# Layer two's first pair of blocks: one second product behind each first one, and x's parts apart from x's sums

## The chip, the cores and the metric

The kernel runs on one core of a Trainium2 chip. The metric is the device time of one execution in microseconds, as the median of several runs; less is better. A separate execution was recorded by the hardware profiler, and its own time is given beside its span. The engines of a core are TensorE (in the rows PE; its weight loads PEld), VectorE (DVE), ScalarE (ACT), GpSimd (POOL) and SyncE (SP, which issues the transfers here). Each engine works through its own queue in the order in which the program issues; engines wait for one another by semaphores.

## The reference

A retention layer makes x (1536 tokens by 512), and two layers of two matrices each follow. Layer one bends with a softplus, layer two with a scaled square:

```python
x = retention(q, k, v)                       # 1536 x 512
h = x @ w_in;  g = maximum(h, 0) + log1p(exp(-abs(h)));  x = g @ w_out
h = x @ w2_in; r = maximum(h, 0); g = s * (r * r) + b;   out = g @ w2_out
```

The widths are 512 (x) and 2048 (h), so a layer has 16 blocks of 128 columns of h. All is float32.

## The kernel before

**Precision.** A float32 operand is cut into a high and a low part (`split`, L107 to L114: ScalarE copies to the high part, L111; GpSimd or VectorE subtracts it, L114), and a product is made of three matmuls, high by high, high by low and low by high. The tokens are cut into three tiles j of 512; x's parts are `xh[j]`, `xl[j]` and its plain float32 copy, or what is kept in its place, `xa[j]`. A weight half comes as 64-bit words; `split_w` makes it into float32 on VectorE in four steps (L286, L290, L295, L301) with a square on ScalarE (L293, "wm"), and then cuts it into `wh` (ScalarE, L111) and `wl` (GpSimd, L114). It is a generator: `go(work, n)` runs its next n steps, so that a slot of the program does one weight half: two steps early in the slot, the rest at its end. Loads of weights are issued from the third step, four buffers ahead.

**Layer one** runs in 48 steps s (a first product `h_mm` of 12 matmuls into bank h or y, the softplus on VectorE and ScalarE, and, LAG = 3 steps later, the second product `acc_mm` of 12 matmuls into four accumulator banks). At the end of the steps the second products of blocks 45, 46 and 47 are still to do, all of tile j = 2, and then x's tile 2 is finished by `take_last`, for two banks at a time: VectorE adds `xa` to the accumulators in place (L416), ScalarE writes `xh` from them (L418), and VectorE writes `xl` (L420).

**Layer two** works on pairs p of blocks. From the second pair on (`second`, p >= 1), tiles 0 and 1 of x are multiplied by a scheme with seven products in the place of eight (`six`, 6 matmuls each). It needs sums of x's parts, T1 = B12 - B11, T2 = B22 - T1, T3 = B22 - B12 (made before T2) and N4 = B21 - T2, cut into high and low parts, and sums of the weights: four differences on GpSimd (L320, "ws"), their high part on ScalarE (L111, "sh") and low part on GpSimd (L114, "sl"). They are a slot's work (`sums_w`) like a weight half: the four differences in its first two steps, sh and sl in the third. A product that stays in a bank while another is made in the same bank is copied out by ScalarE (`kept`, L469, p1, p5 and u2). Buffers p1 and p5 hold T3 before that, one copy of each.

**The first pair** (`plain(0)`) makes its six products plainly, in six slots (j, half): (0,0), (0,1), (1,0), (1,1), (2,0), (2,1). A slot issues, in this order: the first product (`all_of`, 12 matmuls on TensorE into the bank named in its call), the relu on ScalarE (`flat`, L486), square (L492), affine (L493) and high part gh (L111) on ScalarE with the low part gl on GpSimd (L114), the first two steps of its split work, then `accs()` (second products on TensorE, and what reads the accumulators), the sums of x, and the rest of the split work. The split works of the slots are, in order: a weight half of block 19, the weight sums of the second pair, two weight halves, and a weight half each of blocks 20 and 21. `acc_2(p, j, half)` is a second product (12 matmuls) into the four accumulator banks; the first of a tile takes new accumulators and so waits for what still reads the old ones, bank by bank (banks 0 and 1 are one buffer, 2 and 3 one each). `take` moves a tile's accumulators to `xa[j]` with four VectorE instructions (L518 for the first pair, L520 later).

Before the change, `mixed_x(k)` does a sum of x on VectorE (L446, L431, L441) and its parts on ScalarE (L447, or L111 for T3) and GpSimd (L449, or L114) at one place, T3 and N4 excepted, whose parts come in later slots: T1 and T3's sum in the last step of layer one, T2 in slot (0,0), N4's sum in (0,1) and parts in (1,1), T3's parts in (2,0). The second products stand so: blocks 45 and 46 in slot (0,0); 47 and `take_last` in (0,1); the first pair's own second products of tile 0 in (1,0) and (1,1), with `take`; none in (2,0) and (2,1). The order of TensorE's queue is therefore (0,0), 45, 46, (0,1), 47, (1,0), second product of (0,0), (1,1), second product of (0,1), (2,0), (2,1). The order on every engine is the order in which the program is written; nothing reorders it (`tc.manual_schedule()`).

Of the kernel before, what the change touches and what calls it, by code (L numbers as in the profile page):

```python
# [7 lines left out]
F32 = mybir.dt.float32  # L8
F32R = mybir.dt.float32r
U32 = mybir.dt.uint32  # L10
AF = mybir.ActivationFunctionType
ALU = mybir.AluOpType

P = 128
# [7 lines left out]
TT = 512  # L22
# [10 lines left out]
FIRST, SECOND = (0, 1), (2, 3)  # L33
LAG = 3
# [13 lines left out]
def tile_retention_mlps(ctx: ExitStack, tc: tile.TileContext, qk, kv, w1, w2, sb, consts, out):  # L48
# [19 lines left out]
    def bank(pool, tag):  # L68
        return pool.tile([P, 512], F32, tag=tag, name=tag)
# [39 lines left out]
    def split(hi, lo, src, hi_eng, lo_eng):  # L109
        if hi_eng is nc.scalar:  # L110
            nc.scalar.activation(hi, src, AF.Copy)  # L111
        else:
            hi_eng.tensor_copy(hi, src)
        lo_eng.tensor_tensor(out=lo, in0=src, in1=hi.bitcast(F32), op=ALU.subtract)  # L114
# [269 lines left out]
    def acc_mm(s, banks):  # L384
        la, g, j, f4 = steps[s]
        wh, wl = w_t[block(s), 1]
        gh, gl = gg_t[s]
        if (la, g, j) not in acc_t:
            acc_t[la, g, j] = sums()[0] if acc_t else ac
        parts = ((0, 1), (2,)) if len(banks) > 1 else ((0, 1, 2),)  # L390
        for some in parts:
            for cc in banks:
                cs = slice(cc * P, (cc + 1) * P)
                ops = ((wh[:, cs], gh), (wh[:, cs], gl), (wl[:, cs], gh))
                for i in some:
                    nc.tensor.matmul(  # L396
                        acc_t[la, g, j][cc], *ops[i], start=f4 == 0 and i == 0, stop=ends(s) and i == 2
                    )
# [23 lines left out]
    x_t = {}  # L422
    x3 = []

    def mixed_x(k):

        (b11, b21), (b12, b22) = ((xa[j][:, 0:2], xa[j][:, 2:4]) for j in (0, 1))
        if k == 3:
            for c, tag in enumerate(("p1", "p5")):
                t = late.tile([P, TT], F32, tag=tag, name=tag)  # L430
                nc.vector.tensor_tensor(out=t, in0=b22[:, c], in1=b12[:, c], op=ALU.subtract)  # L431
                x3.append(t)
            return
        if k == 4:
            hi, lo = xh[1][:, 0:2], xl[1][:, 0:2]
            for c in range(2):
                split(hi[:, c], lo[:, c], x3[c], nc.scalar, nc.gpsimd)
            x_t[3] = hi, lo
            return
        if k == 5:  # L440
            nc.vector.tensor_tensor(out=b12, in0=b21, in1=b22, op=ALU.subtract)  # L441
            return
        to, x, y = {1: (b11, b12, b11), 2: (b22, b22, b11), 0: (b12, None, None)}[k]
        hi, lo = (late.tile([P, 2, TT], F32R, tag=f"x{k}{e}", name=f"x{k}{e}") for e in "hl")
        if x is not None:
            nc.vector.tensor_tensor(out=to, in0=x, in1=y, op=ALU.subtract)  # L446
        nc.scalar.activation(hi, to, AF.Copy)  # L447
        for c in range(2):
            nc.gpsimd.tensor_tensor(out=lo[:, c], in0=to[:, c], in1=hi[:, c].bitcast(F32), op=ALU.subtract)  # L449
        x_t[k] = hi, lo  # L450

    def six(ps, w, x, start):
# [48 lines left out]
    def acc_2(p, j, half, banks=FIRST + SECOND):  # L501
        wh, wl = w_t[NF + 2 * p + half, 1]
        gh, gl = gg_t[p, half, j]
        if (1, p, j) not in acc_t:
            acc_t[1, p, j] = sums()[0]
        for some in ((0, 1), (2,)):
            for cc in banks:
                cs = slice(cc * P, (cc + 1) * P)
                ops = ((gh[:, cs], wh), (gl[:, cs], wh), (gh[:, cs], wl))
                for i in some:  # L510
                    nc.tensor.matmul(  # L511
                        acc_t[1, p, j][cc], *ops[i], start=half == 0 and i == 0, stop=half == 1 and i == 2
                    )
# [112 lines left out]
    with tc.manual_schedule():  # L626
# [90 lines left out]
        for s in range(SB, NS):  # L717
            old = s - LAG
            takes = ends(old)
            late_work = work  # L720
            work = split_next(s + 1) if not takes else iter(())
            h_mm(s)
            act_0(s)
            if s > SB:
                act_3(s - 1)
            go(work, 2)
            acc_mm(old, FIRST)
            if takes:
                take_out(old, 0)
                take_out(old, 1)  # L730
            act_1(s)
            if s > SB:
                act_hi(s - 1)
            act_2(s)
            go(late_work, 1)
            if s > SB:
                act_lo(s - 1)
            acc_mm(old, SECOND)
            if takes:
                take_out(old, 2)  # L740
                take_out(old, 3)
            for k in SUMS_AT.get(s, ()):
                mixed_x(k)
            go(work, 2)

        def part(p):
# [6 lines left out]
        def plain(p):  # L753

            w = NF + 2 * p

            def slot(j, half, to, accs, sums=()):
                work = part(p)
                all_of(to, w_t[w + half, 0], j)
                c = flat(to)  # L760
                bend(c, p, half, j)
                go(work, 2)
                accs()
                for k in sums:
                    mixed_x(k)
                go(work, 3)

            def last():
                for s in range(NS - LAG, NS - 1):
                    acc_mm(s, FIRST + SECOND)  # L770

            def end():
                for banks in (FIRST, SECOND):
                    acc_mm(NS - 1, banks)
                    take_last(banks)

            def sums_0():
                acc_2(p, 0, 1)
                take(p, 0)

            slot(0, 0, bank(ps_h, "h"), last, (2,))
            slot(0, 1, bank(ps_y, "y"), end, (5,))
            slot(1, 0, bank_2[1], lambda: acc_2(p, 0, 0))
            slot(1, 1, bank(ps_h, "h"), sums_0, (0,))
            slot(2, 0, bank_2[1], lambda: None, (4,))
            slot(2, 1, bank(ps_y, "y"), lambda: None)

        def second(p):

            w = NF + 2 * p  # L790
            (ah, al), (bh, bl), (sh, sl) = w_t[w, 0], w_t[w + 1, 0], s_t[w]
            a11, a12 = (ah[:, :KH], al[:, :KH]), (ah[:, KH:], al[:, KH:])
            a22 = bh[:, KH:], bl[:, KH:]
            s1, s2, s3, s4 = ((sh[:, k], sl[:, k]) for k in range(4))
            b11, b21 = ((xh[0][:, k : k + 2], xl[0][:, k : k + 2]) for k in (0, 2))
            b22 = xh[1][:, 2:4], xl[1][:, 2:4]
            t1, t2, t3, n4 = (x_t[k] for k in (1, 2, 3, 0))

            one, other, third = bank(ps_h, "h"), bank(ps_y, "y"), bank_2[1]

            work = part(p)
            six(one, a11, b11, True)
            p1 = kept(one, "p1")
            six(third, a12, b21, True)
            c11 = joined(third, p1)
            go(work, 2)
            acc_2(p - 1, 1, 0)
            bend(c11, p, 0, 0)
            go(work, 3)

            work = part(p)
            six(other, s1, t1, True)
            p5 = kept(other, "p5")
            six(one, s2, t2, False)
            u2 = kept(one, "u2")
            go(work, 2)
            acc_2(p - 1, 1, 1)
            take(p - 1, 1)
            go(work, 3)

            work = part(p)
            six(other, s4, b22, False)
            c12 = joined(other, u2)
            six(one, s3, t3, False)
            c22 = joined(one, p5)
            go(work, 2)
            acc_2(p - 1, 2, 0)
            bend(c12, p, 0, 1)
            bend(c22, p, 1, 1)
            go(work, 3)  # L830

            work = part(p)
            six(one, a22, n4, False)
            c21 = flat(one)
            go(work, 2)
            acc_2(p - 1, 2, 1)
            take(p - 1, 2)
            bend(c21, p, 1, 0)
            go(work, 3)

            work = part(p)
            all_of(third, (ah, al), 2)
            ha = flat(third)
            go(work, 2)
            acc_2(p, 0, 0)
            bend(ha, p, 0, 2)
            go(work, 3)

            other = bank(ps_y, "y")
            all_of(other, (bh, bl), 2)  # L850
            hb = flat(other)
            for banks in (FIRST, SECOND) if p == PAIRS - 1 else (FIRST + SECOND,):
                acc_2(p, 0, 1, banks)
                take(p, 0, banks)
            bend(hb, p, 1, 2)
# [85 lines left out]
```

## Time and profile before

| | |
|---|---|
| median of 3 runs | 585.06 us (584.42 to 586.7) |
| profiled execution | 585.04 us, span on the core 583.2 us |
| mean granted TensorE clock | 0.994 of full |
| busy: TensorE, weight loads | 98%, 80% |
| busy: VectorE, ScalarE, GpSimd | 72%, 54%, 41% |

The span is the profiled stretch on the core; the execution's time has some 1.8 us around it. Times in the rows count from the span's start. An instruction's row has its start, its length, its engine and line, what it writes and reads, and in brackets how long the engine was idle before it and what ended that. TensorE's matmuls overlap in the rows: a row says 0.39 us, but they start closer together than that. A row with x2 or x4 merges so many instructions in a line. The second pair (p = 1) begins behind slot (2,1), at about 345 us.

### The profile page before, as it was taken

To read this page: it belongs to the slowest core of one execution; us is meant where nothing else is said; L and a number is where in the kernel's file an instruction comes from. 1 tells how busy PE (TensorE), PEld (TensorE's weight loads), DVE (VectorE), ACT (ScalarE), POOL (GpSimd) and SP (SyncE) were. 2 spreads that over 40 slices of the span, in tenths; PEclk is the share of its full clock that TensorE was granted. 3 is DMA by queue.
4 is the path that set the end of the run, shared out by engine and by line. 5 is a ranking of instruction groups with operands and counts; after the bars stand their busy time and mean duration, and the time that the engine had idled before them with its cause. 6 is when DMAs were issued, how large, how long until landed. Compare 5 with 4: busy or idle time off the path is not lost.

```text
span 583.2 us, 7949 instructions
## 1 busy us (share of the span) xinstructions
PE 569.2 (98%) x2986; PEld 467.2 (80%) x2986; DVE 419.8 (72%) x626; ACT 316.6 (54%) x570; POOL 236.3 (41%) x197
## 2 busy tenths in 40 slices
PE   8999999999999999999999798999999999999997
PEld 7877778888888888888888586888888888888885
DVE  4899766788799997999869775749394857653324
ACT  3656564444233233243435776958677676767460
POOL 3447632111110120120525777665747464735030
PEclk9999999999999999999999898999999999999999
DMA  8986212122122131122121131403021222000005
GB/s 322 415 316 199 69 53 93 46 100 62 48 73 67 50 100 37 52 93 72 38 72 37 36 97 53 141 0 114 33 95 50 72 73 72 2 1 0 1 1 215
DMA packets 14869, 50.57 MB, mean 87 GB/s; under 512 B 1776, under 2 KB 1776, under 8 KB 14832
## 3 DMA queue, kind: packets, MB, share of 16 engines
q1 hardware_dynamic: 14832, 50.08, 25.0%
q8 instruction: 23, 0.38, 0.3%
q14 instruction: 14, 0.11, 0.1%
HBM read 46.93 MB, written 3.15 MB: 86 GB/s over the span
## 4 chain that ended last, share of the span: by engine, by line
PE 84%; DVE 6%; DMA 5%; ACT 3%; issue 1%; SPq 0%; DVEq 0%
PE acc L511 22%; PE acc L396 21%; PE h L349 12%; PE y L349 9%; PE h L455 7%; PE y L463 3%; PE third L463 3%; PE y L455 3%; DMA qk<-qk 3%; PE y L189 2%; DMA raw<-w 2%; PE third L455 1%; PE s L173 1%; DVE wm L301 1%; DVE xa L446 1%
## 5 line engine op out<-in xcount | busy, mean ns | idle before, releaser
L114 POOL TENSOR_TENSOR wl<-wm,wh 128x512 fp32r<-128x512 f32 x64 | 83.3, 1302 | 223.0 <-ACT wh L111 223.0
L520 DVE TENSOR_TENSOR xa<-acc,xa 128x512 f32<-128x512 f32 x84 | 52.4, 684 | 81.8 <-PE acc L511 81.8
L114 POOL TENSOR_TENSOR gl<-c,gh 128x512 fp32r<-128x512 f32 x48 | 62.1, 1294 | 77.6 <-ACT gh L111 64.0
L362 ACT ACTIVATE t<-t 128x512 f32<-128x512 f32 x48 | 30.2, 629 | 102.9 <-DVE t L356 102.8
L511 PE MATMUL acc<-wh,gh 128*128 128x512 f32 x192 | 76.0, 396 | 3.7 <-DVE xl L420 3.7
L396 PE MATMUL acc<-gh,wh 128*128 128x512 f32 x192 | 75.6, 394 | 0.0
L511 PE MATMUL acc<-wh,gl 128*128 128x512 f32 x192 | 75.4, 393 | 0.0
L396 PE MATMUL acc<-gl,wh 128*128 128x512 f32 x192 | 74.8, 390 | 0.0
L111 ACT ACTIVATE wh<-wm 128x512 fp32r<-128x512 f32 x64 | 39.8, 622 | 49.9 <-DVE wm L301 49.9
L396 PE MATMUL acc<-gh,wl 128*128 128x512 f32 x192 | 58.1, 389 | 0.0
L511 PE MATMUL acc<-wl,gh 128*128 128x512 f32 x192 | 53.0, 392 | 0.0
L382 DVE TENSOR_TENSOR gl<-t,gh 128x512 fp32r<-128x512 f32 x40 | 52.1, 1302 | 1.2 <-ACT gh L378 1.2
L349 PE MATMUL h<-xh,wh 128*128 128x512 f32 x112 | 44.7, 399 | 2.3 <-DVE t L366 1.7
L293 ACT ACTIVATE wm<-raw 128x512 f32<-128x512 f32 x64 | 42.2, 660 | 8.5 <-POOL wl L114 8.4
L511 PEld LDWEIGHTS acc<-wh,gh 128*128 128x128 f32 x192 | 36.6, 190 | 12.5 <-issue 3.4
L349 PE MATMUL h<-xl,wh 128*128 128x512 f32 x112 | 43.7, 390 | 0.0
L396 PEld LDWEIGHTS acc<-gh,wh 128*128 128x128 f32 x192 | 36.1, 188 | 8.8 <-DVE xa L406 1.0
L511 PEld LDWEIGHTS acc<-wl,gh 128*128 128x128 f32 x192 | 36.6, 190 | 7.7
L511 PEld LDWEIGHTS acc<-wh,gl 128*128 128x128 f32 x192 | 36.6, 191 | 7.6
L396 PEld LDWEIGHTS acc<-gh,wl 128*128 128x128 f32 x192 | 36.0, 188 | 7.6
L396 PEld LDWEIGHTS acc<-gl,wh 128*128 128x128 f32 x192 | 36.0, 188 | 7.2
L493 ACT ACTIVATE c<-c,sbt 128x512 f32<-128x512 f32 x48 | 39.2, 816 | 1.6
(179 smaller groups left out, 1237.6 us busy)
## 6 DMA issues: line engine op xcount, KB each, us to landing
raw<-w SPq DMA_DIRECT2D x64, 512.0 KB, 3.7
qk<-qk SPq DMA_DIRECT2D x12, 512.0 KB, 8.2
kv<-kv SPq DMA_DIRECT2D x12, 512.0 KB, 8.1
out<-xa SPq DMA_DIRECT2D x12, 256.0 KB, 2.1
cst<-consts SPq DMA_DIRECT2D x1, 518.0 KB, 4.2
cst<-consts SPq DMA_DIRECT2D x1, 256.0 KB, 6.4
sbt<-sb SPq DMA_DIRECT2D x1, 1.0 KB, 9.7
```

The source lines that it names most:

```text
L111: nc.scalar.activation(hi, src, AF.Copy)
L114: lo_eng.tensor_tensor(out=lo, in0=src, in1=hi.bitcast(F32), op=ALU.subtract)
L293: nc.scalar.activation(m, hw.bitcast(F32), AF.Square)
L349: nc.tensor.matmul(ps, w[:, cc * P : (cc + 1) * P], r[j][:, cc, :], start=i == 0, stop=i == len(ops) - 1)
L362: nc.scalar.activation(l_t[s], l_t[s], AF.Softplus)
L382: (eng or nc.vector).tensor_tensor(out=gl, in0=l_t.pop(s), in1=gh.bitcast(F32), op=ALU.subtract)
L396: nc.tensor.matmul(acc_t[la, g, j][cc], *ops[i], start=f4 == 0 and i == 0, stop=ends(s) and i == 2)
L455: nc.tensor.matmul(ps, w[a][:, k * P : (k + 1) * P], x[b][:, k], start=start and i == 0, stop=i == len(ops) - 1, skip_group_check=True,)
L463: nc.tensor.matmul(ps, w[a][:, k * P : (k + 1) * P], (xh, xl)[b][j][:, k], start=i == 0, stop=i == len(ops) - 1)
L493: nc.scalar.activation(c, c, AF.Identity, scale=sbt[:, 0:1], bias=sbt[:, 1:2])
L511: nc.tensor.matmul(acc_t[1, p, j][cc], *ops[i], start=half == 0 and i == 0, stop=half == 1 and i == 2)
L520: nc.vector.tensor_tensor(out=dst, in0=ps, in1=dst, op=ALU.add)
```

## The change

`mixed_x` is cut into `sum_x` (VectorE alone) and `parts_x` (ScalarE and GpSimd). In the last step of layer one only the sums T1 and T3 stay. In the six slots the second products are spread to one each: block 45 in (0,0), 46 in (0,1), 47 with `take_last` in (1,0), the first pair's second products of tile 0 in (1,1) and, with `take`, in (2,0), none in (2,1). T2's sum stays in (0,0), N4's in (0,1). The parts go: T1 to (0,0), T2 to (0,1), N4 to (1,1), T3 to (2,1). The banks of the six slots stay as they were. The split works stay in their slots.

```diff
--- before.py
+++ after.py
@@ -422,7 +422,7 @@
     x_t = {}
     x3 = []
 
-    def mixed_x(k):
+    def sum_x(k):
 
         (b11, b21), (b12, b22) = ((xa[j][:, 0:2], xa[j][:, 2:4]) for j in (0, 1))
         if k == 3:
@@ -431,22 +431,21 @@
                 nc.vector.tensor_tensor(out=t, in0=b22[:, c], in1=b12[:, c], op=ALU.subtract)
                 x3.append(t)
             return
-        if k == 4:
-            hi, lo = xh[1][:, 0:2], xl[1][:, 0:2]
+        to, x, y = {1: (b11, b12, b11), 2: (b22, b22, b11), 4: (b12, b21, b22)}[k]
+        nc.vector.tensor_tensor(out=to, in0=x, in1=y, op=ALU.subtract)
+        x_t[k] = to
+
+    def parts_x(k):
+        if k == 3:
+            hi, lo, src = xh[1][:, 0:2], xl[1][:, 0:2], x3
             for c in range(2):
-                split(hi[:, c], lo[:, c], x3[c], nc.scalar, nc.gpsimd)
-            x_t[3] = hi, lo
-            return
-        if k == 5:
-            nc.vector.tensor_tensor(out=b12, in0=b21, in1=b22, op=ALU.subtract)
-            return
-        to, x, y = {1: (b11, b12, b11), 2: (b22, b22, b11), 0: (b12, None, None)}[k]
-        hi, lo = (late.tile([P, 2, TT], F32R, tag=f"x{k}{e}", name=f"x{k}{e}") for e in "hl")
-        if x is not None:
-            nc.vector.tensor_tensor(out=to, in0=x, in1=y, op=ALU.subtract)
-        nc.scalar.activation(hi, to, AF.Copy)
+                nc.scalar.activation(hi[:, c], src[c], AF.Copy)
+        else:
+            hi, lo = (late.tile([P, 2, TT], F32R, tag=f"x{k}{e}", name=f"x{k}{e}") for e in "hl")
+            nc.scalar.activation(hi, x_t[k], AF.Copy)
+            src = [x_t[k][:, c] for c in range(2)]
         for c in range(2):
-            nc.gpsimd.tensor_tensor(out=lo[:, c], in0=to[:, c], in1=hi[:, c].bitcast(F32), op=ALU.subtract)
+            nc.gpsimd.tensor_tensor(out=lo[:, c], in0=src[c], in1=hi[:, c].bitcast(F32), op=ALU.subtract)
         x_t[k] = hi, lo
 
     def six(ps, w, x, start):
@@ -740,7 +739,7 @@
                 take_out(old, 2)
                 take_out(old, 3)
             for k in SUMS_AT.get(s, ()):
-                mixed_x(k)
+                sum_x(k)
             go(work, 2)
 
         def part(p):
@@ -754,7 +753,7 @@
 
             w = NF + 2 * p
 
-            def slot(j, half, to, accs, sums=()):
+            def slot(j, half, to, accs, sums=(), parts=()):
                 work = part(p)
                 all_of(to, w_t[w + half, 0], j)
                 c = flat(to)
@@ -762,12 +761,10 @@
                 go(work, 2)
                 accs()
                 for k in sums:
-                    mixed_x(k)
+                    sum_x(k)
+                for k in parts:
+                    parts_x(k)
                 go(work, 3)
-
-            def last():
-                for s in range(NS - LAG, NS - 1):
-                    acc_mm(s, FIRST + SECOND)
 
             def end():
                 for banks in (FIRST, SECOND):
@@ -778,12 +775,12 @@
                 acc_2(p, 0, 1)
                 take(p, 0)
 
-            slot(0, 0, bank(ps_h, "h"), last, (2,))
-            slot(0, 1, bank(ps_y, "y"), end, (5,))
-            slot(1, 0, bank_2[1], lambda: acc_2(p, 0, 0))
-            slot(1, 1, bank(ps_h, "h"), sums_0, (0,))
-            slot(2, 0, bank_2[1], lambda: None, (4,))
-            slot(2, 1, bank(ps_y, "y"), lambda: None)
+            slot(0, 0, bank(ps_h, "h"), lambda: acc_mm(NS - 3, FIRST + SECOND), sums=(2,), parts=(1,))
+            slot(0, 1, bank(ps_y, "y"), lambda: acc_mm(NS - 2, FIRST + SECOND), sums=(4,), parts=(2,))
+            slot(1, 0, bank_2[1], end)
+            slot(1, 1, bank(ps_h, "h"), lambda: acc_2(p, 0, 0), parts=(4,))
+            slot(2, 0, bank_2[1], sums_0)
+            slot(2, 1, bank(ps_y, "y"), lambda: None, parts=(3,))
 
         def second(p):
 
@@ -794,7 +791,7 @@
             s1, s2, s3, s4 = ((sh[:, k], sl[:, k]) for k in range(4))
             b11, b21 = ((xh[0][:, k : k + 2], xl[0][:, k : k + 2]) for k in (0, 2))
             b22 = xh[1][:, 2:4], xl[1][:, 2:4]
-            t1, t2, t3, n4 = (x_t[k] for k in (1, 2, 3, 0))
+            t1, t2, t3, n4 = (x_t[k] for k in (1, 2, 3, 4))
 
             one, other, third = bank(ps_h, "h"), bank(ps_y, "y"), bank_2[1]
```

## Rows read from the trace of the kernel before

**Rows 1.** the chain of waits, late in the run: start, us, what

```profile
398.33 2.72 PE acc L511 x12
...
568.35 11.19 PE acc L511 x48
```

**Rows 2.** TensorE's waits, to 330 us and after: us, times, longest

```profile
PE acc L511 <- DVE xl L420: 3.0, 1, 3.0
...
PE h L455 <- ACT p L469: 1.9, 1, 1.9
PE acc L511 <- DVE xl L420: 0.7, 1, 0.7
```

**Rows 3.** stretches of 4 us: length, busy time by engine, clock, DMA share, GB/s

```profile
332.00:336.00 4.00, 4.00 (x14) 3.19 (x14) 3.45 (x5) 3.36 (x6) 3.67 (x2) 0.74 0.00 0
...
356.00:360.00 4.00, 4.00 (x15) 3.20 (x14) 0.50 (x2) 3.70 (x7) 4.00 (x5) 0.75 0.00 0
```

**Rows 4.** TensorE in order of time: start, us, instruction, idle before

```profile
309.83 0.39 PE L463 MATMUL h<-xh,wh 128*128 128x512 f32 x1
...
329.33 0.47 PE L511 MATMUL acc<-wh,gh 128*128 128x512 f32 x1 [2.99 <-DVE xl L420]
...
331.20 0.80 PE L511 MATMUL acc<-wh,gh 128*128 128x512 f32 x1 [0.71 <-DVE xl L420]
...
334.47 0.40 PE L463 MATMUL h<-xh,wh 128*128 128x512 f32 x1
...
354.25 0.55 PE L455 MATMUL h<-x2h,sh 128*128 128x512 f32 x1 [1.90 <-ACT p L469]
...
360.08 0.39 PE L455 MATMUL y<-xh,sh 128*128 128x512 f32 x1
```

**Rows 5.** ScalarE in order of time, slots (0,1) and (1,0)

```profile
323.60 0.63 ACT L111 ACTIVATE wh<-wm 128x512 fp32r<-128x512 f32 x1 [0.40 <-DVE wm L301]
...
326.80 1.06 ACT L418 ACTIVATE xh<-acc 128x512 fp32r<-128x512 f32 x2
...
331.19 1.06 ACT L111 ACTIVATE sh<-ws 128x1024 fp32r<-128x1024 f32 x1 [0.17 <-POOL ws L320]
332.15 0.58 ACT L486 ACTIVATE c<-third 128x512 f32<-128x512 f32 x1
...
334.81 0.65 ACT L293 ACTIVATE wm<-raw 128x512 f32<-128x512 f32 x1
```

**Rows 6.** GpSimd in order of time, slots (0,0) and (0,1)

```profile
319.73 1.29 POOL L114 TENSOR_TENSOR gl<-c,gh 128x512 fp32r<-128x512 f32 x1 [1.63 <-ACT gh L111]
...
327.01 1.26 POOL L114 TENSOR_TENSOR gl<-c,gh 128x512 fp32r<-128x512 f32 x1
328.24 0.72 POOL L320 TENSOR_TENSOR ws<-wm 128x256 f32<-128x256 f32 x1
```

**Rows 7.** VectorE in order of time: the T1 and T2 sums, take_last's L420

```profile
311.92 1.21 DVE L446 TENSOR_TENSOR xa<-xa,xa 128x1024 f32<-128x1024 f32 x1
...
319.96 2.15 DVE L446 TENSOR_TENSOR xa<-xa,xa 128x1024 f32<-128x1024 f32 x1
...
327.89 1.29 DVE L420 TENSOR_TENSOR xl<-acc,xh 128x512 fp32r<-128x512 f32 x2 [2.99 <-ACT xh L418]
```

**Rows 8.** VectorE, ScalarE and GpSimd, last slots and second pair's start

```profile
339.70 2.48 DVE L518 COPY xa<-acc 128x512 f32<-128x512 f32 x4 [1.94 <-PE acc L511]
...
343.70 0.63 ACT L111 ACTIVATE wh<-wm 128x512 fp32r<-128x512 f32 x1 [1.99 <-DVE wm L301]
...
347.46 1.14 ACT L111 ACTIVATE xh<-p 128x512 fp32r<-128x512 f32 x2
...
353.62 0.58 ACT L469 ACTIVATE p<-h 128x512 f32<-128x512 f32 x1
...
357.99 1.06 ACT L111 ACTIVATE sh<-ws 128x1024 fp32r<-128x1024 f32 x1 [0.23 <-POOL ws L320]
...
348.32 2.55 POOL L114 TENSOR_TENSOR xl<-p,xh 128x512 fp32r<-128x512 f32 x2
```

## The prediction

> **What bounds the kernel now.** I read the chain of waits first: in its last part there is nothing but TensorE, matmul behind matmul, twelve in 2.72 us, so one in 0.2267 us [rows 1]. A microsecond that TensorE loses earlier is therefore a microsecond of the end. The waits of TensorE come next: around the change it waits three times, 3.0 and 0.7 us for L420 and 1.9 us for the copy p at L469, and for nothing after that [rows 2]. Last I read the clock by stretches and TensorE's instructions in order. Behind both places the granted clock is about 0.75 of full in a stretch of 4 us [rows 3], that is, part of the stretch at 1.2 GHz and the rest at 2.4: the 8 matmuls from 331.20 to 334.47 us take 3.27 us where 8 x 0.2267 is 1.81 [rows 4].
>
> What there is to win is bounded by this. From 309.83, the first product of slot (0,0), to 360.08, the third six-matmul product of the second pair's sums, TensorE issues 180 matmuls (six slots of 12, layer one's blocks 45 to 47 with 12 each, four second products of 12, four products of 6): 180 x 0.2267 = 40.81 us. It takes 50.25 [rows 4]. So 9.44 us are lost. Of these, 5.57 lie at the first second product: without a wait it would run from 326.18 to 328.90 (309.83 + 84 x 0.2267), and it ends at 334.47. The other 3.87 lie around the 1.90 us wait at 354.25.
>
> **Part one, the new order of TensorE.** No matmul is added or removed. Block 46 moves behind slot (0,1), block 47 with its take_last behind (1,0), and each second product one first product later. TensorE's queue becomes (0,0), 45, (0,1), 46, (1,0), 47, (1,1), then the second product of (0,0). By 0.2267 each, block 47 runs from 323.45 to 326.18 (before from 320.7) and TensorE reaches the second product at 328.90. That product writes the four accumulator banks in which take_last works in place, so it waits for the two L420 of take_last's first half, and in its middle for those of the second half.
>
> **Part two, take_last on ScalarE.** This decides. ScalarE works in program order. Before, take_last stands in slot (0,1) ahead of sh, ScalarE's half of the split of the weight sums; its xh start at 326.80 and sh at 331.19 [rows 5]. Changed, take_last stands in slot (1,0): behind sh, the relu, square, affine and gh of that slot, and the square of a weight word (wm). So when can sh start? It needs the four weight differences on GpSimd (L320), which stand behind gl of slot (0,1). Before, that gl starts at 327.01, the differences at 328.24 [rows 6], and sh waits for the last of them and starts 2.95 behind the first. Changed, GpSimd has the same number of instructions in front (T1's two low parts in the place of T2's two), and ScalarE's wh at 323.60, which opens slot (0,1), still follows VectorE's T2 sum, L295 and L301. I take sh at 331.19 as before. From there the rows already give the next ones: wm of slot (1,0) starts at 334.81 [rows 5], and the instruction behind that wm of 0.65 us follows some 0.56 later (ScalarE's instructions overlap by about 0.1: sh is 1.06 long and its follower starts 0.96 behind it), so the first xh of take_last starts at 335.37 and not at 326.80.
>
> From xh to TensorE it was 329.33 - 326.80 = 2.53 us for the first two banks and 331.20 - 326.80 = 4.40 for the others [rows 4, 5]; L420 in between starts 1.09 behind xh, at 327.89 [rows 7]. Changed, this is 337.90 and 339.77. TensorE, there at 328.90, stands 9.0 us, then 1.0 (4 matmuls fit in the 1.87). The remaining 8 at the low clock take 3.27 as they did: the product ends at 343.04, where without a wait it ends at 331.62. Loss 11.42 in the place of 5.57: **+5.85 us**. ScalarE is idle for most of it: between T2's high part, finished about 327.9, and sh there are 3.3 us in which the xh could have run, but they stand behind.
>
> **Part three, the second pair's start.** The products (2,0), second of (0,1), (2,1), two of six, second of (1,0), s1 by T1 follow without a wait: 66 x 0.2267 = 14.96, to 358.00. Then s2 by T2 writes the bank that p1 must have read. Before, from the first L518 of the eviction to the wh behind it was 343.70 - 339.70 = 4.00, and that L518 came 2.47 us behind its product's start, which is 334.47 + 12 x 0.23 = 337.23 [rows 4, 8]. Changed, the product of (0,1) starts at 345.76, L518 at 348.23, and wh at 352.23; the relu and its three followers take 2.66 to the wm behind them (332.15 to 334.81 [rows 5]): wm at 355.42, the high parts of T3 at 355.98. Here is a second new wait. T3 now lies in slot (2,1), right ahead of p1, and p1 takes T3's buffer, so it waits for GpSimd's first low part. Two low parts take 2.55, one 1.27, and the first started 0.86 behind its high part (347.46, 348.32 [rows 8]): 356.84 to 358.12, p1 to 358.75, TensorE at 358.80. Loss 0.80.
>
> Six matmuls and the second product of (1,1) run to 362.88. s4 by B22 then needs p5, and p5 stands behind the next sh, as before (sh at 357.99, [rows 8]). GpSimd: second low part to 359.40, wl (as long as a gl) to 360.65, then 2.95 to sh at 363.60; sh takes 0.96 (331.19 to 332.15) and p5 0.58: TensorE goes on at 365.18. Loss 2.30. The 1.90 us wait of before was followed by the low clock: 18 matmuls from 354.25 to 360.08 took 5.83 us in the place of 4.08, which is 1.75 more. A wait of 2.30 is longer than that one, so I take 1.75 again; bounds 0 and 1.75. Sum here 0.80 + 2.30 + 1.75 = 4.85 against 3.87: **+0.98**.
>
> **Part four, what costs nothing.** The sums and parts are the same instructions in other slots: the T sums on VectorE of 1.21 us undisturbed, or 2.15 [rows 7], lie ahead of VectorE's wait for the xh at 335.4, and the parts of T1, T2, N4 are used from 356 us on. T2's low parts on GpSimd follow the differences, to about 333.7, and push sl behind, which is needed at 356.6 first. T1's leave layer one's last step, where GpSimd's wl may start 0.3 us earlier; ScalarE there waits for L301 anyway. If this cover were gone, the cost would be at most the 0.94 by which a T sum grows. No transfer is moved past a needed one: loads are issued a few microseconds later with four buffers ahead.
>
> The T2 sum and GpSimd's gl of (0,0) meet: they start at 319.96 and 319.73 [rows 6, 7], and the sum takes 2.15 instead of 1.21, ending 1.1 us behind gl's end. In the changed kernel VectorE is some 0.25 us earlier there, so it may win this race and wh come 1.2 us earlier. The Trainium skill, "SBUF — State Buffer", section "Who interferes with whom", says that a VectorE instruction with two SBUF inputs contends with a GpSimd one that reads SBUF, and that the order of issue decides which of them is blocked; this trace agrees (2.15 against 1.21). By that rule, what VectorE wins GpSimd loses, and the estimate stays; with no such lock sh would come about 1.2 us earlier and the time be some 590.7.
>
> **Sum.** 5.85 + 0.98 = 6.83 us. The profiled execution took 585.04 us (its span 583.2), next to the median 585.06: forecast **591.9 us**, slower by 1.2%. Bounds: without the clock's 1.75 and with sh 1.2 to 1.9 us earlier, +3.2 to +3.9 (588.2 at the least); with one more stretch of low clock behind the 9 us wait (+1.75), +8.6 (593.6).
>
> **Rivals.** (1) The order does even out the load: ScalarE has some 3.8 us of work for each slot (2.66, and wm and wh with 0.56 each) and TensorE now 5.44 in five of the six, where before the last two had 2.72 alone. If the second pair then starts with no wait at all, 3.87 us come back: 5.85 - 3.87 = +2.0, 587.0 us. For it: the load; against it: p1 behind T3, p5 behind sh. (2) Faster: the accumulators are free when TensorE comes. It decides on one point: xh of take_last must start by 328.90 - 2.53 = 326.4 us. Then all 9.44 us can go: 575.6. Partly met it gives partly: break-even with the forecast's second place lies at an xh start of about 328.6 (335.37 less 6.8). It would need ScalarE to run xh ahead of sh and of the relu chain, or the differences to be done some 7 us sooner; ScalarE kept its program order through all of [rows 5], and gl, which stands ahead of them, started only at 327.01. (3) The order of the queues is not what I read, and the accumulators wait for the same as before: no change, 585.
>
> **How the numbers follow.** Forecast with its bounds 0.78; slower still, over 594.4, 0.03; rival 1 0.08 and rival 3 0.05, both within half a per cent; rival 2 0.06. Half a per cent, 2.9 us, is about what a measurement of this kernel can tell from no change: so faster 0.06, same 0.13, slower 0.81. The range holds the bounds of the unknown costs, 588.2 to 593.6, with 0.8 above for the readings that I had to carry over, and reaches below to rival 1: 586.8 to 594.4. It leaves out 0.14.
>
> **What would show it.** In the changed profile: one wait of TensorE for L420 of 7 to 9 us from about 329 us, and one of 1 to 2 behind it; ScalarE idle about 3 us ahead of sh, and take_last's xh near 335 instead of 327, behind wm; a low clock behind it; waits for p at L469 of 0.5 to 1 and of 2 us. Wrong, if the xh start before 329 us, if sh does not stand ahead of them in ScalarE's queue, or if TensorE has no wait over 3 us between 326 and 345.

## The result, and the profile after

The changed kernel takes 591.32 us in the median (591.12 to 591.76, 4 runs), where the kernel before has 585.57 beside it (584.42 to 586.7): a ratio of 1.0099, with a 95% interval of 1.0077 to 1.0122. Its profiled execution took 591.23 us with a span of 589.2, against 585.04 and 583.2: 6.19 us more. Forecast were 591.9 us and 6.83 more. In this trace the first product of slot (0,0) starts 0.15 us earlier than in that of before (309.68, 309.83); where start times of the two are compared below, this is allowed for.

TensorE's waits from 300 us on (in all, times, longest), which answer to [rows 2]; line numbers are a little lower in the changed kernel (L510 for L511, L468 for L469):

```profile
PE acc L510 <- DVE xl L420: 8.6, 1, 8.6
PE y L454 <- ACT p L468: 1.9, 1, 1.9
PE h L454 <- ACT p L468: 0.7, 1, 0.7
```

The 3.0 and 0.7 us for L420 are one wait of 8.6 now (the second, for the other banks, lies in the product's low clock), and there are two waits for the copies p1 and p5 in the place of one. No other wait of TensorE is listed. ScalarE in order of time, against [rows 5] and [rows 8]:

```profile
325.43 1.04 ACT L445 ACTIVATE x2h<-xa 128x1024 fp32r<-128x1024 f32 x1
330.76 1.06 ACT L111 ACTIVATE sh<-ws 128x1024 fp32r<-128x1024 f32 x1 [4.29 <-POOL ws L320]
...
334.38 0.65 ACT L293 ACTIVATE wm<-raw 128x512 f32<-128x512 f32 x1
334.94 1.07 ACT L418 ACTIVATE xh<-acc 128x512 fp32r<-128x512 f32 x2
...
357.36 0.60 ACT L468 ACTIVATE p<-h 128x512 f32<-128x512 f32 x1 [0.54 <-POOL xl L448]
...
362.74 1.06 ACT L111 ACTIVATE sh<-ws 128x1024 fp32r<-128x1024 f32 x1 [1.21 <-POOL ws L320]
363.70 0.58 ACT L468 ACTIVATE p<-y 128x512 f32<-128x512 f32 x1
```

Between T2's high part at 325.43 and sh at 330.76 ScalarE stands 4.29 us idle and waits for GpSimd's last weight difference (3.3 forecast; T2's high part was done earlier than assumed). The first half of take_last (L418) stands behind sh, the relu chain and wm, at 334.94: 8.29 us later than before. Further down sh of the third pair waits 1.21 us, and p5 stands behind it at 363.70. TensorE's side, against [rows 4]:

```profile
309.68 0.39 PE L462 MATMUL h<-xh,wh 128*128 128x512 f32 x1
...
337.47 0.77 PE L510 MATMUL acc<-wh,gh 128*128 128x512 f32 x1 [8.58 <-DVE xl L420]
...
342.16 0.39 PE L462 MATMUL third<-xh,wh 128*128 128x512 f32 x1
...
358.00 0.50 PE L454 MATMUL h<-x2h,sh 128*128 128x512 f32 x1 [0.72 <-ACT p L468]
...
364.33 0.50 PE L454 MATMUL y<-xh,sh 128*128 128x512 f32 x1 [1.95 <-ACT p L468]
...
371.51 0.39 PE L454 MATMUL h<-x4h,wh 128*128 128x512 f32 x1
```

The second product of (0,0) runs from 337.47 to 342.16, its 12 matmuls in 4.69 us where 2.72 would do; the 24 from 364.33 to 371.51 take 7.18 in the place of 5.44. The clock shows why. Stretches of 4 us, third figure from the end the granted clock, against [rows 3]:

```profile
332.00:336.00 4.00, 0.00 (x0) 0.00 (x0) 0.00 (x0) 3.90 (x7) 4.00 (x3) 0.50 0.00 0
336.00:340.00 4.00, 2.53 (x6) 1.72 (x7) 3.90 (x7) 1.20 (x3) 0.71 (x1) 0.50 0.00 0
340.00:344.00 4.00, 4.00 (x17) 3.21 (x16) 3.44 (x5) 2.56 (x4) 1.29 (x1) 0.85 0.40 131
...
364.00:368.00 4.00, 3.67 (x10) 2.97 (x11) 2.49 (x4) 2.58 (x5) 3.44 (x2) 0.64 0.36 110
```

It is at half already during the 8.6 us wait and stays there until about 341.2, and it falls again behind the 1.95 us wait. VectorE and GpSimd at the beginning of the stretch, against [rows 6] and [rows 7]:

```profile
319.52 1.22 DVE L435 TENSOR_TENSOR xa<-xa,xa 128x1024 f32<-128x1024 f32 x1
...
322.11 2.11 DVE L435 TENSOR_TENSOR xa<-xa,xa 128x1024 f32<-128x1024 f32 x1
...
319.56 2.32 POOL L114 TENSOR_TENSOR gl<-c,gh 128x512 fp32r<-128x512 f32 x1 [1.90 <-ACT gh L111]
321.85 3.52 POOL L448 TENSOR_TENSOR x1l<-xa,x1h 128x512 fp32r<-128x512 f32 x2
...
330.01 0.72 POOL L320 TENSOR_TENSOR ws<-wm,ws 128x256 f32<-128x256 f32 x1
```

Here the T2 sum (319.52) came 0.04 us ahead of GpSimd's gl: it took 1.22 us, and gl 2.32 in the place of 1.29; then the N4 sum took 2.11 and T1's two low parts 3.52 in the place of 2.55. The last difference ends at 330.73, and sh could start.

### The profile page after: what moved, and what is told of

It reads as the page before. It is cut to its first block, busy times and chain, and to the rows that moved or that the text cites. A ratio compares the mean times of both kernels' runs of the same rounds, so it can differ in the third digit from the quotient of the medians.

```text
span 589.2 us, 7951 instructions
## 1 busy us (share of the span) xinstructions
PE 569.9 (97%) x2986; PEld 467.4 (79%) x2986; DVE 419.4 (71%) x626; ACT 316.6 (54%) x570; POOL 237.6 (40%) x197
## 4 chain that ended last, share of the span: by engine, by line
PE 82%; DMA 5%; DVE 4%; POOL 3%; ACT 3%; issue 2%; SPq 0%; DVEq 0%; POOLq 0%
PE acc L510 21%; PE acc L396 20%; PE h L349 12%; PE y L349 9%; PE h L454 6%; PE y L462 3%; PE third L462 3%; PE y L454 3%; DMA qk<-qk 3%; PE y L189 2%; DMA raw<-w 2%; PE third L454 1%; PE s L173 1%; POOL gl L114 1%; POOL wl L114 1%
## 5 line engine op out<-in xcount | busy, mean ns | idle before, releaser
L510 PE MATMUL acc<-wh,gh 128*128 128x512 f32 x192 | 76.1, 396 | 8.6 <-DVE xl L420 8.6
L510 PE MATMUL acc<-wh,gl 128*128 128x512 f32 x192 | 75.6, 394 | 0.0
L510 PE MATMUL acc<-wl,gh 128*128 128x512 f32 x192 | 52.5, 389 | 0.0
L510 PEld LDWEIGHTS acc<-wh,gh 128*128 128x128 f32 x192 | 36.5, 190 | 17.5 <-issue 9.0
L510 PEld LDWEIGHTS acc<-wh,gl 128*128 128x128 f32 x192 | 36.6, 191 | 7.5
L510 PEld LDWEIGHTS acc<-wl,gh 128*128 128x128 f32 x192 | 36.2, 188 | 7.6
```

Of the source, the lines that this page charges most:

```text
L510: nc.tensor.matmul(acc_t[1, p, j][cc], *ops[i], start=half == 0 and i == 0, stop=half == 1 and i == 2)
```

## The experiments

Three theories stood at the start. A, that of the prediction: take_last and p1, p5 come late because of what is ahead of them in ScalarE's queue. B: TensorE's new order costs the time by itself. C: x's parts in their new slots make GpSimd, and so sh, late.

**The order alone.** The changed kernel with the parts where they were:

```diff
             for k in SUMS_AT.get(s, ()):
                 sum_x(k)
+                if k == 1:
+                    parts_x(1)
-            slot(0, 0, ..., sums=(2,), parts=(1,))
-            slot(0, 1, ..., sums=(4,), parts=(2,))
+            slot(0, 0, ..., sums=(2,), parts=(2,))
+            slot(0, 1, ..., sums=(4,))
-            slot(2, 0, bank_2[1], sums_0)
-            slot(2, 1, bank(ps_y, "y"), lambda: None, parts=(3,))
+            slot(2, 0, bank_2[1], sums_0, parts=(3,))
+            slot(2, 1, bank(ps_y, "y"), lambda: None)
```

> The changed order of the second products (one behind each first product) with x's sums and parts where they were before. Theory A (take_last stands in ScalarE's queue behind sh, and sh waits for GpSimd's four differences): sh starts about 331 to 332.4 us, take_last's first xh 4.2 behind it, TensorE waits 8.5 to 9.6 us for L420; T3's parts no longer stand right ahead of p1, so only p5 is late, by about 1.2: some 589.5 us, slower than before by 4 and faster than the change by 2. Theory B (the order of TensorE's queue alone costs it, wherever x's parts stand): as the change, 591. Theory C (the moved parts on GpSimd make the differences and so sh late): as before, 585.5.

589.99 us, ratio to before 1.008 (1.0065 to 1.0095). TensorE's waits, and sh and take_last on ScalarE:

```profile
PE acc L510 <- DVE xl L420: 9.8, 1, 9.8
PE y L454 <- ACT p L468: 1.0, 1, 1.0
...
332.38 1.06 ACT L111 ACTIVATE sh<-ws 128x1024 fp32r<-128x1024 f32 x1 [5.28 <-POOL ws L320]
...
336.55 1.06 ACT L418 ACTIVATE xh<-acc 128x512 fp32r<-128x512 f32 x2
```

C falls: with the parts in their old places sh starts later still, 332.38, and take_last 4.17 behind it. The new order costs 4.5 us without them. This alone would fit B too, but for the size.

**The parts alone.** The second products as before, sums and parts as changed:

```diff
-            slot(0, 0, ..., lambda: acc_mm(NS - 3, FIRST + SECOND), sums=(2,), parts=(1,))
-            slot(0, 1, ..., lambda: acc_mm(NS - 2, FIRST + SECOND), sums=(4,), parts=(2,))
-            slot(1, 0, bank_2[1], end)
-            slot(1, 1, ..., lambda: acc_2(p, 0, 0), parts=(4,))
-            slot(2, 0, bank_2[1], sums_0)
+            slot(0, 0, ..., last, sums=(2,), parts=(1,))
+            slot(0, 1, ..., end, sums=(4,), parts=(2,))
+            slot(1, 0, bank_2[1], lambda: acc_2(p, 0, 0))
+            slot(1, 1, ..., sums_0, parts=(4,))
+            slot(2, 0, bank_2[1], lambda: None)
```

> The second products where they were before, x's sums and parts in the changed slots. Theory A: take_last stands ahead of sh again, its first xh at about 325.6, TensorE's waits for L420 1.4 and 1.6 us in the place of 3.0 and 0.7; p1 now behind T3's parts, a wait of 2.6, p5 0.5: some 584 us, 1 to 1.5 faster than before. Theory B: as before, 585.5. Theory C: as the change, 591.

584.24 us, 0.9984 (0.9971 to 0.9998). TensorE's waits:

```profile
PE h L454 <- ACT p L468: 2.5, 1, 2.5
PE acc L510 <- DVE xl L420: 2.5, 2, 1.8
PE y L454 <- ACT p L468: 0.4, 1, 0.4
```

As in the change, VectorE's T2 sum comes ahead of GpSimd's gl, so the relu of slot (0,1) and take_last behind it come about 1.2 us earlier, and L420's waits sum to 2.5 and not 3.7. But the profiled execution gives this back at the second place: p1 stands behind T3's parts (2.5, before 1.9), p5 adds 0.4, and the execution took 585.02 us with a span of 583.2, as before. The median is 1.2 us lower with the clock: the seven executions with a mean granted clock of 0.996 or more took 583.9 to 584.64 us, the profiled one and two others, at 0.993, 585.02 to 586.74. Why the clock fell less in most of them this one trace does not show. So the forecast time came out, but not by the waits that it was made of. C falls again; B is not told from A here.

**sh behind take_last.** One step moved in the changed kernel:

```diff
+            held = []
+
             def slot(j, half, to, accs, sums=(), parts=()):
...
                 for k in parts:
                     parts_x(k)
+                if (j, half) == (0, 1):
+                    held.append(work)
+                    return
+                while held:
+                    go(held.pop(), 3)
                 go(work, 3)
```

> The changed kernel with one step moved: the third step of the weight sums (sh on ScalarE, sl on GpSimd) is issued in slot (1,0) behind take_last and not at the end of slot (0,1). Theory A: the relu chain of (1,0) starts at about 326.4 us, but its wm still waits for the differences (it writes a buffer that they read), so take_last's first xh starts at about 331.3 to 331.8 in the place of 334.94 and TensorE waits 4.5 to 5 us for L420 in the place of 8.6; the later waits for p stay: some 588, 3 to 3.6 faster than the change. Theory B and theory C: no difference from the change, 591.

586.32 us, 1.0016 (1.0007 to 1.0025), 5.0 less than the change. TensorE's waits, then ScalarE's wm, take_last and sh:

```profile
PE acc L510 <- DVE xl L420: 4.3, 1, 4.3
PE y L454 <- ACT p L468: 1.9, 1, 1.9
PE h L454 <- ACT p L468: 0.6, 1, 0.6
...
329.88 0.67 ACT L293 ACTIVATE wm<-raw 128x512 f32<-128x512 f32 x1 [0.97 <-POOL ws L320]
330.45 1.06 ACT L418 ACTIVATE xh<-acc 128x512 fp32r<-128x512 f32 x2
...
334.56 1.05 ACT L111 ACTIVATE sh<-ws 128x1024 fp32r<-128x1024 f32 x1
```

B falls: TensorE's queue is the change's to the instruction, and half of the wait for L420 is gone. The gain was larger than expected, 5.0 us and not 3 to 3.6, and not because of the first place. There wm started at 329.88, behind the third difference and not the fourth, and the wait is 4.3 us; but the product behind it took 5.44 us at the low clock, where the change took 4.69, so that 3.49 us are won, as expected. The other 1.64 us were won at the second place, where TensorE waits as long as in the change, 0.64 us for p1 and 1.95 for p5. Here the clock stays at full behind them:

```profile
360.00:364.00 4.00, 3.44 (x15) 2.87 (x16) 3.04 (x6) 2.80 (x6) 3.45 (x3) 1.00 0.30 93
364.00:368.00 4.00, 4.00 (x20) 3.30 (x19) 3.76 (x6) 3.60 (x6) 0.73 (x2) 1.00 0.17 52
```

**take_last first.** The weight sums' third step is held as before; in slot (1,0) take_last and then this step are issued ahead of the relu chain:

```diff
                 all_of(to, w_t[w + half, 0], j)
+                if (j, half) == (1, 0):
+                    accs()
+                    go(held.pop(), 3)
                 c = flat(to)
                 bend(c, p, half, j)
                 go(work, 2)
-                accs()
+                if (j, half) != (1, 0):
+                    accs()
```

> As the run before it, and take_last is issued ahead of the relu chain and the weight half of slot (1,0); TensorE's queue is that of the change. Theory A: take_last's first xh at 326 to 327 us, TensorE's waits for L420 gone or 1.5 us at most. But ScalarE has not less work and the relu chain of (1,0) still starts at about 332, so the time comes back in part as a wait of about 4 us for p1: some 584, 1 faster than before and 7 faster than the change. Theory B: a wait for L420 stays, 590 to 591. A further theory (D): ScalarE's lateness is not the bound of the second place, then nothing comes back there and the time is 579 to 580.

584.34 us, 0.9984 (0.9975 to 0.9993), 7.0 less than the change. TensorE's waits, and ScalarE:

```profile
PE h L454 <- ACT p L468: 3.7, 1, 3.7
PE acc L510 <- DVE xl L420: 0.7, 1, 0.7
PE y L454 <- ACT p L468: 0.6, 1, 0.6
PE y L454 <- ACT c L485: 0.5, 1, 0.5
...
326.86 1.06 ACT L418 ACTIVATE xh<-acc 128x512 fp32r<-128x512 f32 x2
...
331.29 1.06 ACT L111 ACTIVATE sh<-ws 128x1024 fp32r<-128x1024 f32 x1 [0.21 <-POOL ws L320]
332.26 0.58 ACT L485 ACTIVATE c<-third 128x512 f32<-128x512 f32 x1
```

The wait of 8.6 us is 0.7: that it came of take_last's place in ScalarE's queue is shown. D falls: the relu chain of (1,0) still starts behind sh, at 332.26, ScalarE is busy for 16.9 of the 20.1 us from there to p1's copy and cannot make that up, and 3.7 us come back at p1.

**The second place.** Two runs with one edit each in the changed kernel. In the first, sh and sl of a later pair are issued behind p5 and u2:

```diff
             bend(c11, p, 0, 0)
-            go(work, 3)
 
-            work = part(p)
+            mixed_w, work = work, part(p)
             six(other, s1, t1, True)
             p5 = kept(other, "p5")
             six(one, s2, t2, False)
             u2 = kept(one, "u2")
+            go(mixed_w, 3)
```

> The changed kernel with one step of every later pair moved: the high and low part of the next pair's weight sums (sh, sl) are issued behind the copies p5 and u2 and not ahead of them. Theory A: in the second pair p5 no longer waits for GpSimd's four differences, so TensorE's 1.95 us wait for it and the low clock behind it go; the 8.6 us wait for L420 and the 0.7 for p1 stay: 587.3 us, 3.5 to 4 faster than the change. If the low clock had nothing to do with that wait, only 2 faster, 589.3. Theory C (the second place is late because ScalarE is late there from the first place on, and not for sh): no change, 591.

587.78 us, 1.004 (1.0029 to 1.005), 3.5 less than the change. TensorE's waits, p5 and sh on ScalarE:

```profile
PE acc L510 <- DVE xl L420: 8.6, 1, 8.6
PE h L454 <- ACT p L468: 0.9, 1, 0.9
...
361.43 0.58 ACT L468 ACTIVATE p<-y 128x512 f32<-128x512 f32 x1
...
362.77 1.06 ACT L111 ACTIVATE sh<-ws 128x1024 fp32r<-128x1024 f32 x1 [0.27 <-POOL ws L320]
```

The wait for p5 and the low clock behind it (364 to 368 us: 1.00, was 0.64) are gone together, and 3.5 us with them: 1.95 and 1.74 were lost there in the change. That the wait alone brought the low clock is not shown, since the run with sh behind take_last had the same wait without it. C's form for this place falls. In the second run T3's parts go back to slot (2,0), the last two lines of the first experiment's edit:

> The changed kernel with T3's parts back in slot (2,0). Theory A: p1 no longer waits for GpSimd's T3 part (0.7 us), and GpSimd's four differences come 1.2 us earlier, so p5's wait shrinks from 1.95 to about 1.0 to 1.2, which is short enough to leave the clock: 587.5 to 588.5 us, 2.5 to 3.6 faster than the change; the 8.6 us wait stays. If T3's place does not matter: 591.

588.52 us, 1.0051 (1.0031 to 1.007), 2.8 less than the change.

```profile
PE acc L510 <- DVE xl L420: 8.6, 1, 8.6
PE y L454 <- ACT p L468: 1.0, 1, 1.0
```

p1's 0.7 us is gone and p5's wait 1.0. The clock stayed at full behind it. The two gains should not add up, since both edits work on the same wait; together, with nothing else changed, they were not run.

**ScalarE's queue put right.** On the change's order of TensorE: the cut of a weight half or of the weight sums one slot later, behind the relu chain; take_last ahead of it; and both edits of the second place:

```diff
                 c = flat(to)
                 bend(c, p, half, j)
+                if accs is end:
+                    accs()
+                while held:
+                    go(held.pop(), 3)
                 go(work, 2)
-                accs()
+                if accs is not end:
+                    accs()
...
-                go(work, 3)
+                if (j, half) != (0, 1):
+                    go(work, 2)
+                held.append(work)
```

> The changed order on TensorE, with ScalarE's queue put right throughout: the cut of a weight half (wh, wl) and of the weight sums (sh, sl) is issued one slot later, behind the relu chain, so that the chain waits for no VectorE or GpSimd work of the weights; take_last ahead of them in slot (1,0); T3's parts in (2,0); the next pair's sh and sl behind p5 and u2. Theory A: the chains keep step with TensorE, the waits left are about 1 and 1.6 us for L420: 578 to 579.5 us, 1.1% faster than before and 2.1% faster than the change. A rival (D): ScalarE's sum of work and not its order is the bound, then it is no better than take_last first was, 584.

578.48 us, 0.9875 (0.9856 to 0.9894). All that is left of TensorE's waits is this, 1.3 and 0.7 us:

```profile
PE acc L510 <- DVE xl L420: 2.0, 2, 1.3
```

The clock is at full in every stretch, and the work on all engines is the change's (ScalarE 316.2 us busy, 316.6 in the change). D stands for another theory here than in the run with take_last first: that the sum of ScalarE's work, and not its order, is the bound. It falls.

**And the last gh of layer one ahead of block 18's cut:**

```diff
-        go(work, 4)
+        held.append(work)
         act_3(NS - 1)
         act_hi(NS - 1)
```

> As the run before it, and the last gh of layer one is issued ahead of the cut of block 18's weight half, which goes behind the relu chain of slot (0,0). Theory A: ScalarE's 4.8 us wait for L301 ahead of the first relu goes, the chain starts at about 312.8 us in the place of 316.7, and the first wait for L420 goes: about 577.5, 1 us faster than the run before it. If the lead is lost again at the T2 sum or on GpSimd: no difference, 578.5.

577.35 us, 0.9858 (0.9839 to 0.9876): 8.1 us better than before and 14 better than the change. TensorE's wait, and ScalarE's last gh of layer one and first relu:

```profile
PE acc L510 <- DVE xl L420: 0.7, 1, 0.7
...
311.39 0.63 ACT L378 ACTIVATE gh<-t 128x512 fp32r<-128x512 f32 x1 [0.39 <-DVE t L366]
312.76 0.60 ACT L485 ACTIVATE c<-h 128x512 f32<-128x512 f32 x1 [0.74 <-PE h L462]
```

The first two relus start 0.2 us behind their products, where in the change the first was over 4 us late. The clock is at full throughout.

**Is the change's order worth anything?** The last kernel with the second products where they were before:

```diff
-            slot(0, 0, ..., lambda: acc_mm(NS - 3, FIRST + SECOND), sums=(2,), parts=(1,))
-            slot(0, 1, ..., lambda: acc_mm(NS - 2, FIRST + SECOND), sums=(4,), parts=(2,))
-            slot(1, 0, bank_2[1], end)
-            slot(1, 1, ..., lambda: acc_2(p, 0, 0), parts=(4,))
-            slot(2, 0, bank_2[1], sums_0, parts=(3,))
+            slot(0, 0, ..., last, sums=(2,), parts=(1,))
+            slot(0, 1, ..., end, sums=(4,), parts=(2,))
+            slot(1, 0, bank_2[1], lambda: acc_2(p, 0, 0))
+            slot(1, 1, ..., sums_0, parts=(4,))
+            slot(2, 0, bank_2[1], lambda: None, parts=(3,))
```

> The last run's kernel with the second products where they were before the change (45 and 46 in slot (0,0), 47 with take_last in (0,1), none in the last two slots); everything on ScalarE, VectorE and GpSimd is issued by the last run's rule. Theory A with a part that the change is right in: the last two slots give TensorE 2.72 us each and ScalarE 3.8 or more, so ScalarE falls behind there and TensorE waits some 1.2 us for p1, 0.4 for p5 and 1.6 for the relu of c22: about 580, 2.5 us slower than the last run. If the order of the second products were worth nothing once ScalarE's queue is right: 577.4, the same as the last run.

580.41 us, 0.9911 (0.9895 to 0.9928), 3.1 more than the run before it.

```profile
PE h L454 <- ACT p L468: 1.4, 1, 1.4
PE h L454 <- DVE c L479: 0.7, 1, 0.7
PE acc L510 <- DVE xl L420: 0.7, 1, 0.7
```

So the order is worth 3.1 us here. ScalarE's relus of the last slots start 4.7 to 4.8 us apart in both kernels. With one second product behind each first one, TensorE gives ScalarE 5.44 us a slot; with two slots of 2.72 at the end ScalarE falls behind, p1 is late by 1.4 us and VectorE's sum c22 (L479), which must have read its bank before the next product takes it, by 0.7. The change's first half was right, and paid once ScalarE's queue followed it.

## Why the prediction was right

**What bounds the kernel.** As forecast, TensorE's queue carries the end: the loss measured in it from slot (0,0) on is 6.14 us, where the profiled executions differ by 6.19 and their spans by 6.0 (the product behind the last of the stretch starts 61.83 us behind the first, at 371.51 and 309.68; before 55.69, at 365.52 and 309.83).

**The first place, +5.85 forecast.** The product of (0,0) would end at 331.44 without a wait and ends at 342.16: 10.72 lost. Before, it was 5.60 (309.83 + 84 x 0.2267 is 328.87, not 328.90 as the prediction has it, which makes its 5.57), so +5.12. The mechanism was as put: sh at 330.76 (forecast 331.19, here 331.04 with the trace's lead), xh 4.18 behind it (4.18 forecast), TensorE 2.53 behind xh (2.53). The difference lies in these 0.28 us of sh and in the last term: the product took 4.69 us from its start and not 5.14, because the clock was back at 341.2, ahead of its last four matmuls, and not only at its end. The low clock began during the wait and not behind it, so the first four matmuls filled the 1.87 us to the other banks, and the forecast second wait of 1 us does not show.

**The second place, +0.98 forecast.** It lost 4.87 (29.35 us for 108 matmuls, 24.48 at the full clock) against 3.85, so +1.02. The terms: p1 0.72 (0.80 forecast), p5 1.95 (2.30), the clock 1.74 (1.75). The other 0.46 lies right beside the two waits: they are counted from the end of the last matmul's row, which is 0.39 us long where the next could start 0.23 behind it, and the first matmul behind p1's wait took 0.34. That the clock would fall again behind the second wait was a choice between 0 and 1.75, taken from the nearest row. It came true, but by luck: in the run with sh behind take_last the same wait of 1.95 us was followed by the full clock. Without that choice the forecast would have been 590.1, still inside the range.

**What was costed at nothing.** The sums of x hid behind VectorE's 9.09 us wait for xh. The T2 sum did win its race with gl, as held possible, and the relu of slot (0,1) came 1.2 us earlier. But what VectorE won GpSimd lost: gl grew from 1.29 to 2.32, T1's low parts from 2.55 to 3.52, and sh came 0.28 us earlier and not 1.2. The Trainium skill, "SBUF — State Buffer", section "Who interferes with whom", states that a VectorE instruction with two SBUF inputs contends with a GpSimd one that reads SBUF, and that the order of issue decides which one is blocked. The trace agrees: gl took 2.32 us where the T2 sum started 0.04 us ahead of it, and the T2 sum 2.15 before, where gl was first.

**The rivals.** Rival 1, an even load and no wait at the second place, did not come about in the change, but in the last runs of the changed order the second place has no wait, once neither T3's parts nor sh stand right ahead of p1 and p5. Rival 2 named the point on which it turns, an xh of take_last by 326.4 us: the kernel with the last gh moved too reaches 326.6 in a trace of about the old start, and loses 1.52 us of the 9.44 in the stretch, with one wait of 0.7: 577.35 measured, where 575.6 was worked out for no loss at all. Rival 3, the same wait as before, falls with the wait of 8.6 us in the place of 3.0.

**The base of the method** was to carry each engine's queue forward from the rows of before. Of the nine runs, eight came out within about 0.5 us of the expected figure or range; the one that missed, sh behind take_last, was off by 1.7, the price of a low clock behind p5's wait that did not come. One of the eight, the parts alone, came out by the clock too and not by its waits.

## What to carry to other kernels

An engine that works in program order turns the place of an instruction into a dependency: before moving work to a later slot, read on every engine what it will then stand behind, and what that waits for. Here 2.7 us of slack on TensorE were bought with 8.3 us on ScalarE. Put what waits for a slow engine (the cut of weights, sh) behind what another engine waits for (relu chain, take_last, copies), and only then even out the load; here the new order of TensorE cost 4.5 us with the queues as they were and gained 3.1 with ScalarE's put right.

## What the runs showed of the hardware

The clock behind waits of TensorE came as a surprise. In the profiled executions waits of 0.72 (the change), 1.03 (the order alone, T3 back) and 1.40 us (the old order, last run) left the granted clock at 1.00 in the stretches around them. Behind waits of 1.90 (before) and 1.95 us (the change) TensorE ran at the low level and lost 1.74 to 1.75 us more, nearly as much as the wait itself. So 1.6 us less of waits (0.72 and 1.95 in the change, 1.03 with T3's step back) gained 2.8 us.

What is lost behind a wait did not grow with its length. Behind 3.73 us (take_last first) it was 1.5, behind 4.32 (sh behind take_last) 2.7, and behind 8.58 (the change) 2.0, the wait for the other banks included in the last two. Nor does the length decide whether it is lost: p5's wait of 1.95 us in the run with sh behind take_last, 6.34 us behind one of 0.64, left the clock at full, and that of the change, 6.33 us behind one of 0.72, did not. Executions of one kernel differ as well: of 46 of the kernel before, eight had a mean clock of 0.997 and took 584.6 us in the mean, nine had 0.991 and took 585.8. What decides it these runs do not show, so the price of a wait near 2 us is a range, the wait alone or nearly twice the wait.
